# Block attention with a feed-forward layer: q of five blocks loaded by pairs of heads, scores written with a step

## The chip, the cores and the metric

The kernel runs on one core of one Trainium2 chip. The metric is device time in microseconds for one execution, the median of several runs.

## What is computed

Two steps follow one another. Attention with a causal sliding window of 64 positions runs over 8 sequences of 576 tokens with 8 heads of 64. Its output, brought to one row of 512 numbers per token, goes through a feed-forward layer with a squared ReLU. (The weights carry the prefix `moe_`; there are no experts.)

```python
def _attn_ref(q, k, v):                      # each (8, 8, 576, 64), float32
    scores = scale * np.matmul(q, k.transpose(0, 1, 3, 2))
    rel = pos[:, None] - pos[None, :]
    mask = (rel >= 0) & (rel < 64)
    scores = np.where(mask, scores, -1000000000.0)
    ...                                      # softmax over the last axis
    return np.matmul(attn, v)

x = attn_out.transpose(0, 2, 1, 3).reshape(4608, 512)
h = np.maximum(x @ w_in, 0.0)                # w_in (512, 2048)
out = h * h @ w_out                          # w_out (2048, 512)
```

## The kernel before

**Tiling.** The work is cut into nine blocks. Blocks 0 to 7 are the first 512 tokens of the eight sequences; block 8 (`g == B` in the code) collects the last 64 tokens of all of them. Inside a block, attention runs by units of one head pair (`hp` from 0 to 3): two heads of 64 lie side by side on the 128 partitions.

**The way of q and k to the scores.** The loads go through SyncE's queue into float32 pieces of 128 x 512 (tag `st`), a cast makes them fp16 (`p16`), and a transpose puts the 64 numbers of a head on the partitions. There are two forms of this way. Blocks 0 to 2 are loaded by head pair, four neighbouring tokens to a partition, in runs of 1 KB (`load_qk_pair`, line 171); `cast_qk_pair` (line 184) sorts while it casts, `T` (line 248) transposes on TensorE, and the copy at the end of `T` (line 259) puts the tokens back in order. Blocks 3 to 8 are loaded by 128 tokens and all eight heads, in runs of 256 bytes (`load_part`, line 205); `cast_part` (line 218) casts on POOL in order, and `transpose_part` (line 237) is a DMA transpose of 128 x 512, again issued from SyncE. There each of the four transposes of a block brings 128 tokens of all four head pairs into the tile `qT` or `kT`, which is 128 x 4 head pairs x 512 tokens. The key parts `k` and `k2`, the `v` parts and block 8 have the same functions.

**One unit.** `Sc` (line 275) computes the scores of a head pair: eight groups of 64 queries, each against 128 keys, for each of the two heads. That is 16 matmuls of 64 rows x 64 columns. The two heads of a pair use rows 0-63 and 64-127 of the matrix unit and write different banks of PSUM. The weights are the keys, the moving operand is 64 neighbouring columns of `qT`, and the result is a tile of 128 keys x 64 queries. Then ScalarE takes the exponential of 128 x 1024 scores (line 295) in place of the pair of banks, VectorE applies the mask with a minimum (`M`, line 298), TensorE multiplies by v (`AV`, line 305), VectorE divides (`N`, line 322), and `X` (line 331) transposes into the feed-forward layer's input `xT`.

**The order.** It is written out by hand under `tc.manual_schedule()`. From block 1 on, the work of one step is a list of "fill" groups of TensorE work: `F1` (the first product of the next block, line 351) and `F2` or `L2S` (the second product of this block), each of about 0.87 us. `put(i, ...)` hangs the attention of the block after next between them: `Sc` of two units before fill group i, `M` three or four groups later, `AV` six groups after `Sc`. `next_part` (line 744) spreads the loads, casts and transposes of blocks 3 to 8 over these groups: each call loads and casts one part and issues the DMA transpose of the part that was loaded four calls earlier. All loads, transposes and most stores stand in SyncE's one queue, in that order.

Of the kernel before, what the change touches and what calls it, by code (L numbers as in the profile page):

```python
# [15 lines left out]
def kernel(  # L16
# [13 lines left out]
    nc = tc.nc  # L30
    B, H, S, D = q.shape
    NT, DM = out.shape
    DFF = moe_w_in.shape[1]
    P = 128
# [23 lines left out]
    def pair(hp):  # L58
        return slice(2 * hp, 2 * hp + 2)
# [50 lines left out]
    def piece(*key):  # L110
        home = homes.pop(key, None)
        st[key] = (home if home is not None else
                   stp.tile([P, 512], FP32, name="st_" + "".join(str(x)[0] for x in key[:1]), tag="st"))
        return st[key]

    def copy(engine, out, in_):
        if engine is nc.scalar:
            engine.activation(out=out, in_=in_, func=AF.Copy, scale=1.0)  # L118
        else:
            engine.tensor_copy(out=out, in_=in_)  # L120
# [38 lines left out]
    p16 = {}  # L159
    ev, od, qT, kT = {}, {}, {}, {}  # L160

    def new_v(g, half=0):
        ev[g, half] = vpool.tile([P, 4, H, VW], FP16, name="v_ev", tag="ev", bufs=3)
        nc.gpsimd.memset(ev[g, half][:, :, :, D:VW], 1.0 / X_SCALE)
        if g < B:
            od[g] = vpool.tile([P, 3, H, VW], FP16, name="v_od", tag="od", bufs=2)
            nc.gpsimd.memset(od[g][:, :, :, D:VW], 1.0 / X_SCALE)

    def load_qk_pair(g, what, hp):
        src = {"q": q, "k": k}[what]
        nc.sync.dma_start(  # L173
            out=piece(what, g, hp)[:].rearrange("p (h x) -> p h x", h=2),
            in_=src[g, pair(hp), 0:512, :].rearrange("h (p i) d -> p h (i d)", i=4))
# [8 lines left out]
    def cast_qk_pair(g, what, hp, engine):  # L184
        t = p16p.tile([P, 512], FP16, name=f"{what}16", tag=f"{what}16")
        p16[what, g, hp] = t
        copy(engine, t[:].rearrange("p (i h d) -> p h i d", i=4, h=2),
             st[what, g, hp][:].rearrange("p (h i d) -> p h i d", i=4, h=2))
# [11 lines left out]
                 t[of:of + 64, :, c:c + 3, :])  # L200


    SRC = {"q": q, "k": k, "v": v, "k2": k, "v2": v}

    def load_part(g, what, c):
        t = piece(what, g, c)[:].rearrange("p (h d) -> p h d", h=H)
        src = SRC[what]
        if g < B:
            nc.sync.dma_start(out=t, in_=src[g, :, c * P:(c + 1) * P, :].rearrange("h p d -> p h d"))
        elif what == "q":  # L210
            for par in range(2):
                nc.sync.dma_start(out=t[par * 64:(par + 1) * 64],
                                  in_=src[2 * c + par, :, 512:S, :].rearrange("h p d -> p h d"))
        else:
            b = c + (4 if what[-1] == "2" else 0)
            nc.sync.dma_start(out=t, in_=src[b, :, S - P:S, :].rearrange("h p d -> p h d"))

    def cast_part(g, what, c):
        if what[0] == "v":
            half = 1 if what == "v2" else 0  # L220
            if (g, half) not in ev:
                new_v(g, half)
            copy(nc.gpsimd, ev[g, half][:, c, :, 0:D],
                 st[what, g, c][:].rearrange("p (h d) -> p h d", h=H))
            return
        t = p16p.tile([P, 512], FP16, name=f"{what}16", tag=f"{what[0]}16")
        p16[what, g, c] = t
        copy(nc.gpsimd, t[:], st[what, g, c][:])
# [8 lines left out]
    def transpose_part(g, what, c):  # L237
        to = {"q": qT, "k": kT, "k2": kT}[what]
        key = (g, 1 if what == "k2" else 0)
        if key not in to:  # L240
            to[key] = tpool.tile([P, HP, 512], FP16, name=f"{what}T", tag="T")
        nc.sync.dma_start_transpose(out=to[key][:, :, c * P:(c + 1) * P], in_=p16[what, g, c][:])


    pm, av, xs, xT = {}, {}, {}, {}
# [29 lines left out]
    def Sc(g, hp, apart=False, i=0):  # L275
        both = at_ps[i]
        add = (g, hp) in added
        sc = added[g, hp] if add else [both[:, hh, :] for hh in range(2)]
        if (g, hp, "unit") in qT:
            qu, ku = qT[g, hp, "unit"], [kT[g, hp, "unit"]]  # L280
        else:
            qu, ku = qT[g, 0][:, hp, :], [kT[g, i][:, hp, :] for i in range(2) if (g, i) in kT]
        for j in range(8):
            kj = ku[j // 4] if g == B else ku[0]
            ks = P * (j % 4) if g == B else max(0, 64 * (j - 1))
            for hh in range(2):
                r0 = 64 * hh
                nc.tensor.matmul(sc[hh][:, j * 64:(j + 1) * 64], kj[r0:r0 + 64, ks:ks + P],  # L288
                                 qu[r0:r0 + 64, j * 64:(j + 1) * 64], start=not add,
                                 stop=not add or j == 7)  # L290
        p = apool.tile([P, 2, 512], FP16, name="pm", tag="pm", bufs=4)
        pm[g, hp] = p
        for hh in range(2):
            if apart or hh == 0:
                nc.scalar.activation(out=p[:, hh, :] if apart else p[:], in_=sc[hh] if apart else both[:],  # L295
                                     func=AF.Exp, scale=1.0 / float(D) ** 0.5)
# [322 lines left out]
    with tc.manual_schedule():  # L619
# [8 lines left out]
        for hp in range(HP):  # L628
            homes["v", g0, hp] = hsum[:, hp, :]
            if hp == 3:  # L630
                load_v_pair(g0, 0)
            load_qk_pair(g0, "q", hp)
            load_qk_pair(g0, "k", hp)
# [15 lines left out]
        busy(1)  # L649
        add_mask(g0, 0)  # L650
        Sc(g0, 0)
        T(g0, 1)
        busy(1)
        add_mask(g0, 1, i=1)
        T(g0, 2, ps_f1, "f1", engine=dve)
        cast_qk_pair(g0, "k", 3, dve)
        Sc(g0, 1, i=1)
        add_mask(g0, 2)
        busy(1)
        Sc(g0, 2)  # L660
        T(g0, 3, engine=dve)
        for hp in range(HP):
# [23 lines left out]
        for hp in range(2):  # L686
            load_qk_pair(g1, "q", hp)
            load_qk_pair(g1, "k", hp)
# [55 lines left out]
        def next_part():  # L744

            if parts_left:
                g, w, c = parts_left.pop(0)
                load_part(g, w, c)
                cast_part(g, w, c)
                if w[0] != "v":  # L750
                    pending.append((g, w, c))
                elif g < B and c == 3:
                    shift_v_parts(g)
                behind = len(load_list) - len(parts_left) - 1
            else:
                behind = len(load_list) + 99
            while pending and behind - load_list.index(pending[0]) >= 4:
                transpose_part(*pending.pop(0))
# [52 lines left out]
        for n in range(1, NBLK):  # L811
            g = seq[n]
# [113 lines left out]
```

## Time and profile before

| | |
|---|---|
| Median of 3 runs | 296.46 us (296.03 to 297.95) |
| Profiled execution | 298.29 us, span 296.6 us, granted clock 1.00 |
| TensorE busy | 287.0 us, 97% of the span |
| VectorE, ScalarE, POOL busy | 76%, 60%, 43% |
| Score matmuls from `qT` (L288) | 384 of 64 rows x 64 columns, 190 ns each from start to end |
| Loads of q, k and v for blocks 3 to 7 (L209) | 20 each, 256 KB |
| DMA transposes (L242) | 24 of q, 24 of k, 4 of k2; 3.6 us to land (median) |

The span runs from the first to the last instruction of the profiled execution; its time holds some more before and behind it. Matmuls are pipelined, so the 190 ns of one score matmul are its latency; what one costs in a row of them is the distance between their starts. A busy share says nothing of waits by itself, so the stretches of the run and the timeline have to be read with it.

### The profile page before, as it was taken

What the parts mean: (1) busy time and instruction counts of PE and PEld (TensorE: products, weight loads), DVE (VectorE), ACT (ScalarE), POOL (GpSimd) and SP (SyncE); (2) the same over time, 40 slices, a digit from 0 to 9 for tenths busy, and PEclk for the clock granted to TensorE, in tenths of its full rate; (3) what the DMA queues carried; (4) which work ended last, traced back from release to release, by engine and by line L of the source; (5) the groups of instructions that cost most, each with busy time, mean ns of one, the idle gap of its engine ahead of it and who ended that gap; (6) DMA issues with size and microseconds to landing.
All of it is one profiled execution on the core that took longest, in us unless ns stands there. A gap on an engine that the chain in (4) does not pass through costs nothing.

```text
span 296.6 us, 7511 instructions
## 1 busy us (share of the span) xinstructions
PE 287.0 (97%) x2953; PEld 185.0 (62%) x2953; DVE 225.5 (76%) x395; ACT 178.1 (60%) x308; POOL 126.7 (43%) x215
## 2 busy tenths in 40 slices
PE   7889999999999999999999999999999999999994
PEld 5443445555545456666666666666666666888883
DVE  3667637679877788888778878887798889878781
ACT  3556667598465756575656465646564655687821
POOL 4567868973494358228416722923223000000002
PEclk9999999999999999999999999999999999999999
DMA  7899999999999997999899999899998014201015
GB/s 203 227 314 389 404 356 253 314 252 169 185 259 171 201 206 114 213 185 242 161 210 214 209 158 237 171 198 193 201 220 222 4 27 100 87 5 73 0 73 142
DMA packets 143651, 56.07 MB, mean 189 GB/s; under 512 B 127712, under 2 KB 136160, under 8 KB 143616
## 3 DMA queue, kind: packets, MB, share of 16 engines
q1 hardware_dynamic: 143232, 55.00, 86.0%
q0 software_dynamic: 144, 0.39, 0.6%
q8 instruction: 23, 0.38, 0.6%
q10 hardware_dynamic: 240, 0.20, 0.3%
q14 instruction: 12, 0.10, 0.1%
HBM read 38.80 MB, written 9.44 MB: 163 GB/s over the span
## 4 chain that ended last, share of the span: by engine, by line
PE 88%; SPq 6%; DMA 4%; POOL 1%; ACT 0%; issue 0%; DVE 0%
PE hps L358 34%; PE chain L446 14%; PE side L446 12%; PE ops L394 5%; PE at L480 4%; PE at L318 4%; DMA wsum<-in_moe_w_in_dram 4%; PE at L288 3%; PE side L394 2%; PE chain L394 2%; SPq L180 2%; PE more L446 2%; SPq L173 2%; PE at L344 2%; PE at L446 1%; PE tr L257 1%
## 5 line engine op out<-in xcount | busy, mean ns | idle before, releaser
L362 ACT ACTIVATE h<-hr 128x512 f16<-128x512 f32 x128 | 80.1, 630 | 80.0 <-DVE hr L361 79.6
L358 PE MATMUL hps<-xT,w_in_sb 128*128 128x512 f16 x496 | 122.7, 379 | 0.6 <-POOL w_in_sb L120 0.4
L361 DVE TENSOR_SCALAR hr<-hps 128x512 f32<-128x512 f32 x127 | 85.8, 686 | 31.3 <-PE hps L358 28.2
L358 PEld LDWEIGHTS <-w_in_sb 128*128 128x128 f16 x500 | 46.7, 98 | 43.2 <-issue 1.4
L446 PEld LDWEIGHTS <-hsum 128*128 128x128 f16 x448 | 43.0, 98 | 11.8
L120 POOL CAST v_ev<-st_v 128x512 f16<-128x512 f32 x31 | 22.3, 720 | 43.6 <-DMA st_v<-in_v_dram 43.6
L446 PEld LDWEIGHTS <-h 128*128 128x128 f16 x336 | 32.7, 98 | 8.3 <-issue 0.4
L120 POOL CAST k<-st_k 128x512 f16<-128x512 f32 x33 | 21.2, 644 | 36.6 <-DMA st_k<-in_k_dram 34.0
L295 ACT ACTIVATE pm<-at 128x1024 f16<-128x1024 f32 x35 | 34.1, 1015 | 2.2 <-PE at L288 2.2
L387 POOL DMA_DIRECT2D out_dram<-osb x3 | 1.8, 596 | 63.2 <-ACT osb L562 61.8
L328 DVE TENSOR_TENSOR xs<-at,rden 128x512 f16<-128x512 f32 x36 | 24.9, 691 | 1.2
L302 DVE TENSOR_TENSOR pm<-pm,mask 128x1024 f16<-128x1024 f16 x32 | 24.1, 765 | 2.0 <-ACT pm L295 1.9
L422 DVE TENSOR_TENSOR hsum<-h 128x1024 f16<-128x1024 f16 x28 | 21.6, 770 | 5.2 <-ACT h L362 5.1
L446 PE MATMUL chain<-wsum,hsum 128*128 128x256 f16 x192 | 24.9, 273 | 0.0
L233 POOL CAST v_od<-st_v 64x512 f16<-64x512 f32 x30 | 22.6, 755 | 1.6
L120 POOL CAST q<-st_q 128x512 f16<-128x512 f32 x28 | 19.2, 709 | 6.1 <-DMA qT<-q 3.5
L394 PEld LDWEIGHTS <-h 128*128 128x128 f16 x128 | 11.6, 98 | 12.2
L318 PEld LDWEIGHTS <-pm 128*64 128x64 f16 x576 | 11.2, 110 | 6.9 <-DVE pm L302 3.0
L118 ACT ACTIVATE xT<-at 128x512 f16<-128x512 f16 x22 | 12.8, 587 | 4.0 <-PE at L344 4.0
L394 PE MATMUL ops<-w_out_sb,h 128*128 128x512 f16 x64 | 14.8, 380 | 0.0
L318 PE MATMUL at<-v_ev,pm 128*64 128x65 f16 x384 | 13.7, 198 | 0.2 <-ACT v_ev L118 0.2
L562 ACT ACTIVATE osb<-chain 128x256 f32<-128x256 f32 x36 | 13.4, 372 | 0.3 <-PE chain L446 0.3
(118 smaller groups left out, 386.2 us busy)
## 6 DMA issues: line engine op xcount, KB each, us to landing
st_k<-in_k_dram SPq DMA_DIRECT2D x37, 256.0 KB, 3.9
out_dram<-osb SPq DMA_DIRECT2D x32, 256.0 KB, 3.1
st_q<-in_q_dram SPq DMA_DIRECT2D x29, 256.0 KB, 4.7
st_v<-in_v_dram SPq DMA_DIRECT2D x28, 256.0 KB, 4.1
w_st<-in_moe_w_in_dram SPq DMA_DIRECT2D x4, 512.0 KB, 6.2
wsum<-in_moe_w_in_dram SPq DMA_DIRECT2D x4, 512.0 KB, 10.2
hsum<-in_moe_w_out_dram SPq DMA_DIRECT2D x4, 512.0 KB, 7.9
wsum<-in_moe_w_out_dram SPq DMA_DIRECT2D x4, 512.0 KB, 9.2
```

What stands on the lines that cost most here:

```text
L120: engine.tensor_copy(out=out, in_=in_)
L233: nc.gpsimd.tensor_copy(out=od[g][to:to + 64, m, :, 0:D], in_=st["v", g, c][of:of + 64, :].rearrange("p (h d) -> p h d", h=H))
L295: nc.scalar.activation(out=p[:, hh, :] if apart else p[:], in_=sc[hh] if apart else both[:], func=AF.Exp, scale=1.0 / float(D) ** 0.5)
L302: nc.vector.tensor_tensor(out=p[:], in0=p[:], in1=m.unsqueeze(1).broadcast_to([P, 2, 512]), op=ALU.min)
L318: nc.tensor.matmul(a[jj * 64:(jj + 1) * 64, hh, jp * VW:jp * VW + D + 1], pm[g, hp][:, hh, j * 64:(j + 1) * 64], vsel, start=True, stop=True)
L328: nc.vector.tensor_tensor(out=x[:].rearrange("p j h d -> p h j d"), in0=a[:, :, :, 0:D], in1=rden[:].unsqueeze(3).broadcast_to([P, 2, 4, D ...
L358: nc.tensor.matmul(hps[:], w_in_sb[:, c, f * P:(f + 1) * P], xT[g][:, c, :], start=(c == 0), stop=(c == DMC - 1))
L361: nc.vector.tensor_scalar(out=hr[:], in0=hps[:], scalar1=0.0, scalar2=None, op0=ALU.max)
L362: nc.scalar.activation(out=h2[g][:, f, :], in_=hr[:], func=AF.Square)
L394: nc.tensor.matmul(f2[g, ts][:], h2[g][:, f, ts * P:(ts + 1) * P], w_out_sb[:, f, :], start=(f == 0), stop=(f == FFC - 1))
L422: (engine or nc.vector).tensor_tensor(out=out, in0=a, in1=b, op=op)
L446: nc.tensor.matmul(to, a[:, f, :], b[:, f, :], start=start and f == 0, stop=f == HF - 1, skip_group_check=True)
```

## The change

For blocks 3 to 7, q is loaded by head pairs with four tokens to a partition, in the form that blocks 0 to 2 already have, and cast by the function that goes with it, on POOL. The DMA transpose then yields one whole head pair: 128 partitions (two heads of 64) x 4 x 128, where the first of the two free dimensions is the token's place among its four neighbours (`i`) and the second the group of four (`p`). Token 4p + i stands in column 128i + p. Nothing puts the tokens back in order; instead `Sc` reads the 64 queries of a group as 4 runs of 16 neighbouring columns, and writes result 16i + p to column 4p + i of the score tile. In the new file, `Sc`'s matmul is line 302 (was 288), `load_qk_pair`'s load line 175 (was 173), and `transpose_part`'s transpose line 250 (was 242). Block 8, k and v are loaded as before, and the number of instructions on every engine stays the same.

```diff
     def load_part(g, what, c):
+        src = SRC[what]
+        if g < B and what == "q":
+            load_qk_pair(g, what, c)
+            return
         t = piece(what, g, c)[:].rearrange("p (h d) -> p h d", h=H)
...
     def cast_part(g, what, c):
...
+        if g < B and what == "q":
+            cast_qk_pair(g, what, c, nc.gpsimd)
+            return
         t = p16p.tile([P, 512], FP16, name=f"{what}16", tag=f"{what[0]}16")
...
     def transpose_part(g, what, c):
...
-        nc.sync.dma_start_transpose(out=to[key][:, :, c * P:(c + 1) * P], in_=p16[what, g, c][:])
+        t = to[key]
+        nc.sync.dma_start_transpose(out=t[:, c, :].rearrange("r (i p) -> r i p", i=4) if g < B and what == "q" else t[:, :, c * P:(c + 1) * P],
+                                    in_=p16[what, g, c][:])
...
     def Sc(g, hp, apart=False, i=0):
...
+        four = g < B and (g, hp, "unit") not in qT
         for j in range(8):
...
-                nc.tensor.matmul(sc[hh][:, j * 64:(j + 1) * 64], kj[r0:r0 + 64, ks:ks + P],
-                                 qu[r0:r0 + 64, j * 64:(j + 1) * 64], start=not add,
-                                 stop=not add or j == 7)
+                to, qj = sc[hh][:, j * 64:(j + 1) * 64], qu[r0:r0 + 64, j * 64:(j + 1) * 64]
+                if four:
+                    to = to.rearrange("s (p i) -> s i p", i=4)
+                    qj = qu[r0:r0 + 64].rearrange("r (i p) -> r i p", i=4)[:, :, 16 * j:16 * j + 16]
+                nc.tensor.matmul(to, kj[r0:r0 + 64, ks:ks + P], qj, start=not add, stop=not add or j == 7)
```

More of the change, by code (lines that the diff above doesn't have):

```diff
@@ L167, in new_v @@
             nc.gpsimd.memset(od[g][:, :, :, D:VW], 1.0 / X_SCALE)
+    SRC = {"q": q, "k": k, "v": v, "k2": k, "v2": v}
     def load_qk_pair(g, what, hp):
-        src = {"q": q, "k": k}[what]
+        src = SRC[what]
         nc.sync.dma_start(
@@ L200, in shift_v_pair @@
                  t[of:of + 64, :, c:c + 3, :])
-    SRC = {"q": q, "k": k, "v": v, "k2": k, "v2": v}
     def load_part(g, what, c):
+        src = SRC[what]
+        if g < B and what == "q":
+            load_qk_pair(g, what, c)
+            return
         t = piece(what, g, c)[:].rearrange("p (h d) -> p h d", h=H)
-        src = SRC[what]
         if g < B:
```

## The prediction

> **What bounds the kernel now.** I read the page's first part, then the chain that ended last, then the stretches, and only then single rows.
>
> ```profile
> PE 287.0 (97%) x2953; PEld 185.0 (62%) x2953; DVE 225.5 (76%) x395; ACT 178.1 (60%) x308; POOL 126.7 (43%) x215
> ...
> PE 88%; SPq 6%; DMA 4%; POOL 1%; ACT 0%; issue 0%; DVE 0%
> ```
>
> TensorE is busy 97% of the span and 88% of the last chain is TensorE; the loads (SPq, DMA) are a tenth of it. Busy shares can hide waits, so the stretches come next. The first changed instruction is the load of block 3's q, issued at 57.92 us; the last changed score matmul belongs to block 7, before 216 us.
>
> ```profile
> 58.00:74.00 16.00, 16.00 (x167) 8.32 (x165) 13.35 (x24) 14.02 (x22) 9.41 (x16) 1.00 1.18 223
> 74.00:108.00 34.00, 34.00 (x337) 17.41 (x337) 25.84 (x41) 19.97 (x32) 17.15 (x27) 1.00 1.14 201
> 108.00:142.00 34.00, 34.00 (x349) 22.64 (x348) 29.56 (x50) 19.88 (x37) 21.12 (x31) 1.00 1.01 190
> ...
> sum 187.00, PE 187.00 PEld 117.33 DVE 152.75 ACT 114.28 POOL 84.10; mean PE 31.17 PEld 19.56 DVE 25.46 ACT 19.05 POOL 14.02
> ```
>
> The columns are the stretch, its length, then PE, PEld, DVE, ACT and POOL busy with their counts, the granted clock, the DMA share and GB/s. The rows left out go on to 245 us, and the last line sums all six. TensorE (the first busy figure) has no idle time in any of them, at a clock of 1.00, while the DMA share stands above 1: transfers queue up, and nobody on TensorE waits for them. So the test is whether TensorE also runs at its pace. The timeline of block 3's first two scores answers that:
>
> ```profile
> 85.39 0.64 PE L288 MATMUL at<-qT,kT 64*128 64x64 f16 x32
> 85.96 1.90 PE L358 MATMUL hps<-xT,w_in_sb 128*128 128x512 f16 x8
> 87.70 1.03 PE L394 MATMUL chain<-w_out_sb,h 128*128 128x512 f16 x4
> ...
> 107.14 1.04 PE L446 MATMUL chain<-w_out_sb,h 128*128 128x256 f16 x8
> 108.01 1.89 PE L358 MATMUL hps<-xT,w_in_sb 128*128 128x512 f16 x8
> ```
>
> Columns are start and duration in us. Eight matmuls of 512 columns go from 85.96 to 87.70: 217 ns each. Eight of 256 columns go from 107.14 to 108.01: 109 ns each. Both are 0.42 ns per column, so 64 columns are worth 27 ns. The 32 score matmuls last 0.64 us, of which the last one's own 0.19 us (below) is its way through the array: the 32nd starts 0.45 us after the first, 15 steps of a pair, 30 ns per pair. A pair is one head in rows 0-63 and one in rows 64-127. So the two run side by side, and a pair costs what one stream of 64 columns costs. TensorE is bound by columns streamed, here too: whatever lengthens the scores lengthens the kernel one for one, and whatever shortens a load does not shorten it.
>
> **The change part by part.** Counts: five blocks (3 to 7) of four head pairs make 20 loads of q, 20 casts, 20 DMA transposes and 20 scores of 16 matmuls: 320 matmuls, 160 side-by-side pairs. The order of instructions on every engine stays; only shapes change.
>
> *Loads.* The old form moves 8 x 64 floats to a partition in runs of 256 bytes, the new 2 x 256 in runs of 1 KB. Both forms are in the trace.
>
> ```profile
> 48.58 0.46 SPq L173 DMA_DIRECT2D hsum<-in_q_dram  x1
> ...
> 81.76 1.15 SPq L209 DMA_DIRECT2D st_q<-in_q_dram  x2
> ```
>
> The new form (L173) holds SP's queue 0.46 us, the old (L209) 1.15/2 = 0.58 us. That is 0.1 us less in each of 20 issues, 2.4 us of SP in all, spread over 104 us (57.9 to 161.6) and worth something only if somebody waits; TensorE does not. Value 0. It cannot be a cost: the bytes are the same and the queue is shorter.
>
> *Casts.* POOL now permutes while it casts, as it already does for blocks 0 to 2:
>
> ```profile
> 57.26 0.61 POOL L120 CAST q<-hsum 128x512 f16<-128x512 f32 x1
> ...
> 65.40 0.62 POOL L120 CAST q<-st_q 128x512 f16<-128x512 f32 x1 [0.52 <-DMA st_q<-in_q_dram]
> 69.55 0.62 POOL L120 CAST q<-st_q 128x512 f16<-128x512 f32 x1 [3.53 <-DMA qT<-q]
> ```
>
> The permuted cast takes 0.61 us, the plain one 0.62. Value 0, 20 times.
>
> *A moved wait.* Buffers of the fp16 q are assigned a little differently in the built program: in block 3 the third and the fourth cast each wait for an earlier transpose of q, where before only the fourth did (the 3.53 us above). The second transpose was issued at 67.33 us and transposes there land after 3.3 to 5.2 us, so the fourth cast can come at up to 72.5 us instead of 69.55. Behind it on POOL stand four casts of k, behind its transpose on SP the loads of v and the transposes of k, and the score waits for the last of these. That one was issued at 79.87 us and landed 3.3 us later, at 83.2; the score began at 85.39. The first k cast would move from 70.11 to 73.1 us, and its transpose from 73.39 to about 75, so the last would land 1.6 to 2.0 us later, within the 2.2 us of cover. Value 0; if the cover is exceeded, up to 0.5 us, once. Block 4's last transpose (103.93 us, landing after at most 4.6) has 6.5 us of cover before the score at 115.05.
>
> *Transposes.* The same 20, each now into one contiguous row of a partition instead of four runs of 128 elements. The trace has only the old destination (3.3 to 5.2 us to land near block 3). Between a gain nobody would see and a loss inside the cover just named: 0.
>
> *Scores.* Each of the 320 matmuls now reads its 64 queries as 4 runs of 16 neighbours (32 bytes a run) and writes its results with a step of 4 floats. No matmul in the trace writes with a step, so the cost has to be bounded by the nearest rows: reads of PSUM by the engines beside it.
>
> ```profile
> L288 PE MATMUL at<-qT,kT x352: 190/190/200, 85.4 to 243.0; 64*128 64x64 f16 x176
> ...
> L295 ACT ACTIVATE pm<-at 128x1024 f16<-128x1024 f32 x35 | 34.1, 1015 | 2.2 <-PE at L288 2.2
> L118 ACT ACTIVATE qk<-tr 128x1024 f16<-128x1024 f16 x7 | 7.1, 1015 | 6.0 <-PE tr L257 6.0
> L120 DVE COPY qk<-tr 128x1024 f16<-128x1024 f16 x4 | 4.9, 1221 | 2.7 <-PE tr L257 2.7
> L295 ACT ACTIVATE pm<-sc 128x512 f16<-128x512 f32 x2 | 1.1, 594 | 1.1 <-PE sc L288 1.1
> ```
>
> L118 reads PSUM permuted (line 259: neighbours lie 128 elements apart) and takes 1015 ns, exactly what L295 takes for the same count read in order. So stepping costs ScalarE nothing: the **lower bound is 0**. A gain is excluded, since the pair already runs at the 30 ns of its columns. But ScalarE handles an element in (1015 - 594)/512 = 0.82 ns, half TensorE's pace of one in 0.42 ns; the row shows that PSUM keeps up with single, scattered elements at 0.82 ns, not faster. VectorE's permuted copy takes 1221/1024 = 1.19 ns. The **upper bound** is that pace with the pair no longer side by side: 64 x 1.19 + 3 = 79 ns a matmul, 158 a pair, 128 more than now, times 160 = 20.5 us. (The 3 ns are the 30 of a pair less the 27 of its columns.)
>
> I take ScalarE's pace, the nearest, with the pair still side by side, because its two matmuls write two different banks: 64 x 0.82 + 3 = 55.6 ns a pair, 25.6 more than now; 160 x 25.6 = **4.1 us**. Score by score this is 0.41 us more for each of ten pairs of units. Nothing hides it. Exp, mask and AV follow the score five groups of matmuls later, and those move along.
>
> [...]
>
> **Sum.** 0 + 0 + 0 + 0 + 4.1 us. The profiled execution's span is 296.6 us and its time 298.29, 1.7 us around the span; with the change 300.7 and 302.4. That execution lies 1.8 us above the median of the runs shown (296.46, from 296.03 to 297.95), so against the median the forecast is 300.6 us, 1.4% more.
>
> **The rivals.**
>
> *Not slower: the stepped write runs at the stream's pace.* Place: L288 (now L302). For it: 1015 ns read in order and 1015 ns permuted. Against it: that pace is half of what is needed. It decides if a pair still takes 30 ns. Price 0, and with the shorter loads at most the off-pace remainder of TensorE before 74 us, under 2 us: 295 to 297, most likely 296.5.
>
> *The write pays for the span that it covers, or the pair loses its side-by-side run.* 64 floats with a step of 4 cover 256; at the 109 ns of a 256-column matmul a pair costs 79 ns more, times 160 = 12.6 us. If instead both keep ScalarE's pace but follow one another, a pair is 111 ns, 81 more, 13.0 us. For it: two streams share one matrix unit, and nothing here shows two slow writers at once. Against it: two banks, and ScalarE's read pays nothing for its span. Time 309.1 to 309.5.
>
> *Both together.* 218 ns a pair, 188 more: 30 us, 326.5.
>
> *Faster, because the queues empty.* The DMA share above 1 speaks for it; TensorE's 187.00 busy us of 187.00 between 58 and 245 us speak against it. Under 2 us in any case.
>
> **How the numbers follow.** Forecast (4.1 us) 0.52, not slower 0.14, span or one after another 0.24, both 0.07, faster 0.03. The likeliest's own range is 299.4 to 302: ScalarE's pace to doubled columns, half a microsecond of moved wait, and the runs' own scatter. The whole range reaches from the not-slower case to the dearer one, 296.0 to 309.8, and leaves out the last. One per cent, about what a measurement of this kernel can tell from no change, is 3 us. Slower by more: the dear cases and nine tenths of the forecast, 0.78. Within: the not-slower case and the rest, 0.19. Faster by more: 0.03.
>
> **What would show it.** In the changed profile the timeline row of two scores (x32 at L302) should read about 1.05 us instead of 0.64, and the next matmul should start 0.98 us after it instead of 0.57. 0.64 again means the first rival, 1.9 the second. POOL's q casts should stay at 0.61 to 0.62 us, and TensorE should show no idle before block 3's first score; a gap there would be the moved wait. A growth that is not in L302's rows would make the working wrong even if the time came out right.

## The result, and the profile after

The changed kernel is slower: 301.48 us (median of 4 runs, 300.31 to 302.56) against 297.20 us for the kernel before beside it (296.03 to 298.53), a ratio of 1.0145 (95% interval 1.0109 to 1.0182). That is 4.3 us.

The page's first part and its chain, after (PE is TensorE's matmuls, PEld its weight loads, DVE VectorE, ACT ScalarE, POOL GpSimd, SPq SyncE's queue):

```profile
PE 290.6 (97%) x2953; PEld 188.6 (63%) x2953; DVE 224.8 (75%) x395; ACT 179.5 (60%) x308; POOL 125.3 (42%) x215
...
DMA packets 128291, 56.07 MB, mean 188 GB/s; under 512 B 107232, under 2 KB 120800, under 8 KB 128256
...
PE 88%; SPq 5%; DMA 4%; POOL 1%; ACT 0%; issue 0%; DVE 0%
```

TensorE's matmuls gain 3.6 us of busy time and its weight loads as much, with the same number of instructions; the shares of VectorE, ScalarE and POOL fall or stay. The loads did change. The row of packets before was:

```profile
DMA packets 143651, 56.07 MB, mean 189 GB/s; under 512 B 127712, under 2 KB 136160, under 8 KB 143616
```

So there are 15,360 packets fewer, 768 for each of 20 loads (1,024 of 256 bytes became 256 of 1 KB).

The stretches (PE busy is the first figure after the length):

```profile
58.00:74.00 16.00, 16.00 (x180) 8.43 (x178) 13.72 (x25) 13.56 (x21) 8.96 (x15) 1.00 1.02 205
74.00:108.00 34.00, 34.00 (x306) 17.51 (x305) 25.24 (x38) 19.78 (x32) 16.34 (x28) 1.00 1.04 207
108.00:142.00 34.00, 34.00 (x345) 22.94 (x344) 28.17 (x49) 19.05 (x34) 20.52 (x31) 1.00 0.89 185
...
sum 187.00, PE 187.00 PEld 118.37 DVE 149.11 ACT 112.07 POOL 81.50; mean PE 31.17 PEld 19.73 DVE 24.85 ACT 18.68 POOL 13.58
```

TensorE is still never idle here. DMA's share (the figure before the last) drops in each of the three stretches shown, by 0.10 to 0.16; of the three left out it drops in two and rises in one (176 to 210 us, from 1.11 to 1.25). In the same 187 us TensorE gets through fewer matmuls (1,935 in the six stretches, before 1,996), and VectorE falls from 152.75 to 149.11 us busy: less work reaches the other engines, and TensorE waits for none of them.

The timeline of block 3's first two scores:

```profile
83.38 1.07 PE L302 MATMUL at<-qT,kT 64*128 64x64 f16 x32
84.38 1.90 PE L370 MATMUL hps<-xT,w_in_sb 128*128 128x512 f16 x8
86.11 1.03 PE L406 MATMUL chain<-w_out_sb,h 128*128 128x512 f16 x4
```

From the first score to the next matmul it is 1.00 us, before 0.57. The extra 0.43 us over 16 pairs is 27 ns a pair, which is what 64 columns cost: a pair takes 56 ns instead of 29 (so far apart are the starts in the two traces; the prediction's 30 came from rounded figures), the pace is halved, and the two heads still run side by side. The matmuls behind are as fast as ever (8 in 1.73 us). All ten such rows of the trace last 1.07 us, where all ten before lasted 0.64; together they make 4.3 us, the whole difference.

The spans of the two profiled executions differ by only 2.2 us (298.8 and 296.6). Their start-up ran differently (why was not traced), and the execution after was 2.0 us ahead before its first changed instruction: a matmul of the first product that starts at 54.23 us before starts at 52.21 us after, and the first changed load follows at 57.47 us. The scores of blocks 0 to 2, which the change does not touch, still have this lead, first before, then after:

```profile
L288 PE MATMUL at<-qk x176: 190/190/238, 6.7 to 74.4; 64*128 64x64 f16 x176
```

```profile
L302 PE MATMUL at<-qT,kT x352: 190/243/243, 83.4 to 245.2; 64*128 64x64 f16 x176
L302 PE MATMUL at<-qk x176: 190/190/200, 6.7 to 72.4; 64*128 64x64 f16 x176
```

The last unchanged score starts at 72.4 us instead of 74.4; the last score of all at 245.2 instead of 243.0. From 2.0 us ahead to 2.2 behind is 4.2 us. The median in the first row of the second fence has risen from 190 to 243 ns: the latency of one matmul has grown too.

### The profile page after: what moved, and what is told of

It is laid out like the page before. It is cut to its first block, busy times and chain, and to the rows that moved or that the text cites. A ratio compares the mean times of both kernels' runs of the same rounds, so it can differ in the third digit from the quotient of the medians.

```text
span 298.8 us, 7513 instructions
## 1 busy us (share of the span) xinstructions
PE 290.6 (97%) x2953; PEld 188.6 (63%) x2953; DVE 224.8 (75%) x395; ACT 179.5 (60%) x308; POOL 125.3 (42%) x215
## 4 chain that ended last, share of the span: by engine, by line
PE 88%; SPq 5%; DMA 4%; POOL 1%; ACT 0%; issue 0%; DVE 0%
PE hps L370 34%; PE chain L458 14%; PE side L458 11%; PE ops L406 5%; PE at L302 5%; DMA wsum<-in_moe_w_in_dram 4%; PE at L492 4%; PE at L330 4%; PE side L406 2%; PE chain L406 2%; PE more L458 2%; SPq L182 2%; PE at L356 2%; SPq L175 2%; PE at L458 1%; SPq L132 1%
## 5 line engine op out<-in xcount | busy, mean ns | idle before, releaser
L120 POOL CAST v_ev<-st_v 128x512 f16<-128x512 f32 x31 | 21.0, 677 | 44.4 <-DMA st_v<-in_v_dram 44.4
L434 DVE TENSOR_TENSOR hsum<-h 128x1024 f16<-128x1024 f16 x28 | 20.4, 729 | 5.2 <-ACT h L374 5.1
L120 POOL CAST q<-st_q 128x512 f16<-128x512 f32 x28 | 20.0, 740 | 6.3 <-DMA qT<-q 5.6
L118 ACT ACTIVATE xT<-at 128x512 f16<-128x512 f16 x22 | 12.8, 586 | 4.0 <-PE at L356 4.0
```

The source lines that it names most:

```text
L434: (engine or nc.vector).tensor_tensor(out=out, in0=a, in1=b, op=op)
```

## The experiments

The open question was where the halved pace comes from: the write with a step, as the forecast had it, or the read in four runs; what exactly is priced; and what the shorter loads are worth alone.

**Read only.** The step in the write is taken away, all else is as in the changed kernel.

```diff
-                    to = to.rearrange("s (p i) -> s i p", i=4)
+                    to = to.rearrange("s (i p) -> s i p", i=4)
```

> Loads, casts, transposes and the strided read of the changed kernel; only the step in the write is taken away (score columns of blocks 3 to 7 come out in the order i, p, so tokens within a group of 64 are mixed up). Theory A, the write to PSUM sets the pace: 32 score matmuls take 0.64 us again and the next matmul starts 0.57 us after the first, and the time is that of the kernel before (ratio 0.997 to 1.003), since the shorter loads hide behind TensorE. Rival B, the read in four runs of 16 sets the pace: 1.07 us and 1.00 us, ratio 1.014. Rival C, half of the cost comes from each: about 0.85 us, ratio 1.007.

297.12 us (10 runs) against 297.21 us (13 runs), ratio 0.9993 (0.9970 to 1.0015). The timeline:

```profile
84.35 0.64 PE L302 MATMUL at<-qT,kT 64*128 64x64 f16 x32
84.92 1.90 PE L370 MATMUL hps<-xT,w_in_sb 128*128 128x512 f16 x8
```

0.57 us, as before the change. So a read in runs of 16 neighbours (32 bytes) is free, and so is everything else in the change: shorter loads, permuted casts, transposes to one row and the moved wait together change the time by something between -0.3% and +0.15%. Theory A held; B and C fell.

**Write only.** The kernel before, with a stepped write of its in-order scores.

```diff
+                if g < B and (g, hp, "unit") not in qT:
+                    to = to.rearrange("s (p i) -> s i p", i=4)
+                    qj = qj.rearrange("r (i p) -> r i p", i=4)
```

> The kernel before with its loads and its read in order, but results of the scores of blocks 3 to 7 written with a step of 4 floats (they come out in another order within a group of 64). Theory A (write): 1.07 us for 32 score matmuls, 1.00 us to the next matmul, 4.27 us more in all. Rival B (read): 0.64 us, 0.57 us, nothing more.

```profile
83.31 1.07 PE L292 MATMUL at<-qT,kT 64*128 64x64 f16 x32
84.31 1.90 PE L360 MATMUL hps<-xT,w_in_sb 128*128 128x512 f16 x8
```

1.00 us to the next matmul, and 301.28 us in its one run, 4.1 us above the median of 297.21 beside it. The next row of scores, at 95.10 us, lasts 1.07 us as well, and the median of the matmuls from `qT` and `kT` is 243 ns, as in the changed kernel. With the read-only kernel beside it, the stepped write alone makes the whole cost.

**What is priced in the write.** Four kernels vary the place of the results alone; loads and read are those of the kernel before. (They ran once each, beside one run of the kernel before at 296.70 us, and after the kernels of "Order by the read instead of the write" below: the 63 ns in the next expectation are from there.) First, runs of two neighbouring floats, 4 floats apart:

```diff
+                    to = to.rearrange("s (p a b) -> s a p b", a=2, b=2)
+                    qj = qj.rearrange("r (a p b) -> r a p b", a=2, b=2)
```

> The kernel before (old loads, read in order), scores of blocks 3 to 7 written in runs of two neighbouring floats with a step of 4 floats between runs (they come out in another order within a group of 64). Theory A1, what counts is that two results in a row lie in one aligned pair of floats: 29 ns a pair of heads, 0.64 us for 32 matmuls, 0.57 us to the next. Rival A2, any step in the write halves the pace: 56 ns, 1.07 us, 1.00 us. With A1 the 63 ns a pair of the run before last (runs of two in the write, alternating read) are the read's.

```profile
83.59 0.64 PE L292 MATMUL at<-qT,kT 64*128 64x64 f16 x32
84.16 1.90 PE L360 MATMUL hps<-xT,w_in_sb 128*128 128x512 f16 x8
```

Free: 0.57 us to the next, and 296.83 us. Then steps of 2 and of 16, with `i=2` and `i=16` in place of `i=4`:

> The kernel before, scores of blocks 3 to 7 written with a step of 2 floats (another order within a group of 64). Theory A1 (one result to a pair of floats costs as much as two): 56 ns a pair of heads, as with a step of 4; 1.07 us and 1.00 us. Rival S (the price goes with the span covered): no more than half of the step of 4's extra, about 42 ns and 0.85 us, or nothing.

```profile
83.67 1.07 PE L292 MATMUL at<-qT,kT 64*128 64x64 f16 x32
84.67 1.90 PE L360 MATMUL hps<-xT,w_in_sb 128*128 128x512 f16 x8
```

> The kernel before, scores of blocks 3 to 7 written with a step of 16 floats (four in a row to places 64 bytes apart, then the next four; another order within a group of 64). Theory A1: again 56 ns a pair of heads, 1.07 us and 1.00 us, whatever the step. Rival S (span, or few places hit again and again): over 56 ns; at the span's price up to four times the step of 4's extra, 135 ns a pair, over 2.2 us for 32.

```profile
84.84 1.07 PE L292 MATMUL at<-qT,kT 64*128 64x64 f16 x32
85.84 1.90 PE L360 MATMUL hps<-xT,w_in_sb 128*128 128x512 f16 x8
```

1.00 us each, the same as with a step of 4; the times are 301.14 and 302.17 us. (The second execution already reached its first changed score 1.2 us later than the first, so their difference is not the scores'.) From 2 to 16 floats the distance has no price; the prediction's rival of the span covered is out. Last, 64 neighbours that begin one float later:

```diff
+                    if j < 7:
+                        to = sc[hh][:, j * 64 + 1:(j + 1) * 64 + 1]
```

> The kernel before, 64 neighbouring results as before, but those of blocks 3 to 7 start one float later in seven of eight groups of queries (the scores stand one column off). Theory A1 in its strict form, two results must fill one aligned pair: each two straddle two pairs, 56 ns a pair of heads in seven of eight, about 1.01 us for 32 matmuls. In its loose form, neighbours merge wherever they start: 33 pairs of floats instead of 32, 29 to 30 ns, 0.64 to 0.66 us.

```profile
83.07 0.65 PE L292 MATMUL at<-qT,kT 64*128 64x64 f16 x32
83.65 1.90 PE L360 MATMUL hps<-xT,w_in_sb 128*128 128x512 f16 x8
```

0.58 us instead of 0.57, and 296.24 us. The loose form holds: 33 pairs of floats instead of 32 would make 0.83 ns (27 ns / 32) more for each of 14 changed pairs of heads, 0.01 us. All these rows fit one estimate: two results in a row that go to neighbouring floats cost 0.83 ns together (29 ns for a pair of heads, 0.57 us to the next matmul, in runs of 64 and of two alike), and a result without such a neighbour costs as much alone (56 ns, 1.00 us, at steps of 2, 4 and 16). Whether aligned pairs are what counts was not shown, since only the 0.01 us of the odd start bears on it; runs of two from an odd float, each across two such pairs, would be the harder test, and no run has them.

**Another shape.** The first product of block 4, 128 rows and 512 columns, accumulating, no second stream beside it.

```diff
+            to, x = hps[:], xT[g][:, c, :]
+            if g == 4:
+                to, x = to.rearrange("s (p i) -> s i p", i=4), x.rearrange("r (i p) -> r i p", i=4)
```

> The kernel before with the first feed-forward product of block 4 alone (16 groups of 4 matmuls of 128 rows x 512 columns, accumulating) written with a step of 4 floats and read in order; its 512 tokens come out in another order for the first layer. Theory A1, 0.83 ns for every write that fills only one of two neighbouring floats, whatever the shape: 64 matmuls at 430 ns instead of 217, 13.6 us more in all (TensorE stays the bound, the other engines have room). Rival E, an accumulating write has to read first and pays more than twice: over 600 ns each, over 25 us more. Rival F, one stream alone (the scores were two side by side) has room to spare: 217 ns, nothing more.

The timeline of this kernel, and then that of the kernel before at the same kind of place:

```profile
135.93 1.88 PE L361 MATMUL hps<-xT,w_in_sb 128*128 128x512 f16 x4
137.60 1.08 PE L449 MATMUL chain<-w_out_sb,h 128*128 128x256 f16 x8
138.52 1.88 PE L361 MATMUL hps<-xT,w_in_sb 128*128 128x512 f16 x4
```

```profile
140.37 1.03 PE L358 MATMUL hps<-xT,w_in_sb 128*128 128x512 f16 x4
141.24 1.04 PE L446 MATMUL chain<-wsum,hsum 128*128 128x256 f16 x8
142.11 1.03 PE L358 MATMUL hps<-xT,w_in_sb 128*128 128x512 f16 x4
```

Four stepped matmuls and eight plain ones take 2.59 us (135.93 to 138.52) instead of 1.74: 0.85 us more for four, 213 ns each, so 430 instead of 217. One run gave 310.75 us against 296.19, 14.6 us more where 13.6 were expected; one run each, with the scatter of the start-up in both, cannot be read closer. Twice the time, in accumulation and in a single stream as well: A1 holds, E and F fall.

**Order by the read instead of the write.** Two kernels keep the results where the changed kernel puts them, but stream the queries so that neighbours are written one after the other. The first alternates between two of the four runs and writes runs of two floats:

```diff
-                    to = to.rearrange("s (p i) -> s i p", i=4)
-                    qj = qu[r0:r0 + 64].rearrange("r (i p) -> r i p", i=4)[:, :, 16 * j:16 * j + 16]
+                    to = to.rearrange("s (p a b) -> s a p b", a=2, b=2)
+                    qj = qu[r0:r0 + 64].rearrange("r (a b p) -> r a p b", a=2, b=2)[:, :, 16 * j:16 * j + 16, :]
```

> The changed kernel with the same results in the same places, but streamed in another order: the query stream alternates between two of the four runs, so that two results in a row go to neighbouring floats and only then does the write step on by 4. Theory A1, a write of two neighbouring floats costs what one alone costs: a pair of heads is back at 29 ns, 32 matmuls 0.64 us, ratio to the kernel before 0.997 to 1.003. Rival A2, any step in the write halves the pace: 56 ns a pair, 1.07 us, ratio 1.014. Rival D, the read, which now jumps 256 bytes with every element, takes over as the bound: 56 ns or more, so this run alone would not tell A2 from D, but the next one does.

Ratio 1.0190 (1.0154 to 1.0226). That interval overlaps the changed kernel's, but the row below, at 1.17 us against 1.07, shows a higher price than the change's own. The second takes one element from each of the four runs in turn and writes 64 neighbours:

```diff
+                    to = to.rearrange("s (p i) -> s p i", i=4)
+                    qj = qu[r0:r0 + 64].rearrange("r (i p) -> r p i", i=4)[:, 16 * j:16 * j + 16, :]
```

> The changed kernel with the tokens put in order by the read instead of the write: the query stream takes one element from each of the four runs in turn (a jump of 256 bytes each), and the results go to 64 neighbouring floats. Theory A with a read that does not care: 29 ns a pair, 0.64 us for 32, ratio to the kernel before 0.997 to 1.003. [...]

Ratio 1.0408 (1.0372 to 1.0443). The rows, one fence a kernel:

```profile
84.30 1.17 PE L302 MATMUL at<-qT,kT 64*128 64x64 f16 x32
85.40 1.90 PE L370 MATMUL hps<-xT,w_in_sb 128*128 128x512 f16 x8
```

```profile
83.56 1.94 PE L302 MATMUL at<-qT,kT 64*128 64x64 f16 x32
85.43 1.90 PE L370 MATMUL hps<-xT,w_in_sb 128*128 128x512 f16 x8
```

1.10 and 1.87 us to the next matmul: 0.53 and 1.30 us more over 16 pairs, so 63 and 111 ns a pair. In the second the results go to 64 neighbouring floats, as in the kernel before, so the 111 ns are the read's. In the first, runs of two might still have played a part, so the read was run alone:

```diff
-                    to = to.rearrange("s (p i) -> s i p", i=4)
+                    to = to.rearrange("s (a p b) -> s a p b", a=2, b=2)
```

> The changed kernel's loads and the alternating read of the runs-of-two kernel (every element 256 bytes from the one before), but results written to 64 neighbouring floats in the order of the stream (tokens within a group of 64 mixed up). If the read alone made that kernel's 63 ns a pair: 63 ns again, 1.17 us for 32 matmuls, 1.10 us to the next. If it needs the stepped write of runs of two as well: 29 ns, 0.64 us.

```profile
84.24 1.17 PE L302 MATMUL at<-qT,kT 64*128 64x64 f16 x32
85.34 0.82 PE L370 MATMUL hps<-xT,w_in_sb 128*128 128x512 f16 x3
```

Again 1.10 us, and 303.26 us against 296.19 (one run each): the 63 ns are the read's alone, and rival D of the first is what happened in both. Why four places (111 ns) cost more than two (63 ns) is open: in both, every element lies about 256 bytes or more from the one before it. Neither of the two reads that order the tokens was free, nor was the stepped write (56 ns). One place was not tried: leave the scores in the order i, p and put them in order where ScalarE reads them for the exponential. Since the loads, casts and transposes alone bring nothing (0.9993), even a free ordering would at best have met the kernel before.

## Why the prediction was right

- **What bounds the kernel.** Right. TensorE had no idle time to lose, so 0.43 us per pair of units went through to the end one for one.
- **Loads, casts, transposes.** Right at 0, by the read-only kernel's 0.9993. The load's issue measured 0.97/2 = 0.49 us where 0.46 was assumed; the median cast over all q pieces is 612 ns, where it was 611 (the slowest 1.14 us in both); the transposes of q land after 3.4 us in the median, as before.

```profile
79.29 1.22 SPq L250 DMA_TRANSPOSE kT<-k  x1
...
81.19 0.97 SPq L175 DMA_DIRECT2D st_q<-in_q_dram  x2
```

- **The moved wait.** Right that it comes and that its cover holds. POOL's rows show both waits for a transpose, and the fourth cast late:

```profile
68.14 0.61 POOL L120 CAST q<-st_q 128x512 f16<-128x512 f32 x1 [4.55 <-DMA qT<-q]
69.86 1.14 POOL L120 CAST q<-st_q 128x512 f16<-128x512 f32 x1 [1.10 <-DMA qT<-q]
```

  The last transpose of k was issued at 79.29 us and landed 3.3 us later, at 82.6; the score began at 83.38. Of 2.2 us of cover 0.8 were left, so 1.4 were used, a little under the 1.6 to 2.0 worked out. TensorE did not stall; another 0.8 us would have used up the cover.
- **The scores.** Right that the stepped write sets the pace and that nothing hides it, and nearly right in size: 25.6 ns a pair were forecast, 27 measured; 4.1 us, 4.3 measured. Where the forecast took its size from is partly luck. It borrowed ScalarE's 0.82 ns for an element, which is close to the 0.83 ns that a stepped result costs TensorE. But the 0.82 ns come from L295's two rows, which read in order, so they say nothing of a step; what TensorE pays goes by pairs of floats, as the runs of two show (0.57 us to the next matmul, against 1.00 for single floats at the same step). The range also counts on doubled columns, an estimate that no row of the kernel before shows; the changed kernel had 56 ns a pair for 29, and 4.3 us.
- **ScalarE's permuted read at 1015 ns** stood for the rival of no cost, and could not carry it. ScalarE takes 0.82 ns for an element in order already, and TensorE's stream brings one every 0.42 ns, so what slows TensorE need not show there. The two rows compared also differ in more than the order: the elements read at L118 are fp16, those at L295 float32.
- **The bounds.** The upper bound of 20.5 us lies under the price of the prediction's own rival of both together, 30 us, so it was no bound.
- **Side by side.** Assumed, and shown: 56 ns a pair, not 111. That the two different banks are the reason was not tried.

## What to carry to other kernels

Before a permutation is moved into a matmul's operand patterns, look at two innermost runs, that of the results and that of the moving operand. Here single results at steps of 2, 4 and 16 floats took twice the time per column (56 ns for 29 in the scores, and 430 for 217 in the product of 512 columns, tried at a step of 4), and neighbouring pairs of floats took no more than before (0.57 us to the next matmul). In the moving operand runs of 16 were free (0.57 us), and single elements taken in turn from two or four places cost two to four times (63 and 111 ns for 29). When TensorE is busy without a gap, read the pace in its starts and not in its busy share, and price each change by columns; a lighter queue elsewhere bought nothing here (0.9993), since TensorE did not wait for it.

## What was not expected of the hardware

- A read that alternates between two places 256 bytes apart costs a pair of heads 63 ns, between four 111 ns, where runs of 16 cost 29: the read's penalty can exceed the write's (56 ns).
- An odd start costs next to nothing (0.65 instead of 0.64 us for 32 matmuls): neighbours share their cost from an odd float on, too.
- ScalarE's pace per element and TensorE's pace per stepped result agree to a hundredth of a nanosecond (0.82 and 0.83); whether that is more than chance, no run here shows.
